# One kernel, two plans: W_in block 3 of the first pair moved to the split path, W_out low parts built by SyncE copies and adding transfers

## The chip, the cores and the metric

The kernel runs on one core of one Trainium2 chip. The metric is the device time of one execution in microseconds (us); before the change it is 329.56 us, the median of three runs (329.25 to 329.67). The engines are TensorE (PE in the profile; PEld are its weight loads), VectorE (DVE), ScalarE (ACT), GpSimd (POOL) and SyncE (SP), which does nothing here but issue transfers. Each engine works through its own instructions strictly in the order in which the program lists them; engines wait for each other by semaphores.

## The reference

A Mamba-2 scan over 4 batches, 8 heads and 768 steps is followed by a feed-forward block with SiLU over the 3072 resulting rows. Everything is fp32.

```python
# scan, per batch and head, in chunks of 32 steps
L = np.exp(cum[:, :, :, None] - cum[:, :, None, :]) * causal
M = np.einsum('bhin,bhjn->bhij', Cc, Bc) * L
y_intra = np.einsum('bhij,bhjd->bhid', M, xc)
y_inter = np.einsum('bhin,bhnd->bhid', Cc, state) * np.exp(cum)[:, :, :, None]
y[:, :, sl] = y_intra + y_inter
state = decay_full[:, :, None, None] * state + np.sum(Bx, axis=2)
...
# feed-forward, x: (3072, 256), w_in: (256, 2048), w_out: (2048, 256)
h = x @ w_in
g = h * (1.0 / (1.0 + np.exp(-h)))
out = g @ w_out
```

## The kernel before

**Units and pairs.** The 3072 rows are cut into 12 units `u` of 256 steps (three for each batch). The scan runs unit by unit; two units make a pair `P` or `G`, and the feed-forward block runs pair by pair, on 512 columns at a time.

**An order written out by hand.** The whole program is one list of entries, `SCHEDULE`, read from left to right: a name and up to four numbers, looked up in `DO` and called. An entry appends its instructions to the lists of its engines. So the list sets the order on each engine, and the order between engines only where data is handed over. A second table, `SLOTS`, says which buffer of a pool each new tile takes; a tile that takes a used buffer has to wait for the last reader of the tile before it. There is no scheduler that could move anything later.

**The weights.** `W_in` and `W_out` are each cut into eight blocks of 256 features; blocks 0 to 7 are W_in, 8 to 15 are W_out. A block is loaded (`lw`) as raw bits, and ACT (`u`, `v`), DVE (`w`, three steps) and POOL (`W`) make an fp32 tile of it (`WT`, 128 x 512). For the fast path a block is split into three tiles: a high part (`H`, ACT), a low part and a third part. The low part is "high + WT". For ten blocks DVE adds it up (`lD`, line 326). For the other six (10 to 15) ACT first copies the high part into a new tile (`Wl`, line 335), and then a transfer issued by POOL adds WT to it in place (`Wm`, line 339, `accum_op=ALU.add`). The third part is made by DVE (`dD`) or by ACT and a second adding transfer (`Wd`, `We`).

**Two ways through the matrix products.** In the split path a product is three sums of TensorE passes over fp32r tiles, each instruction one record in the trace: `a` (high and low parts, 8 records, into PSUM bank `ga` for even blocks and `gb` for odd ones), then ACT scales that bank (`ax`), then `d` (third part, 4 records), then ACT applies SiLU (`dg`). `h` (ACT), `l` and `e` (DVE) split the activations, and `q` is the second product (one `q` is three records). In the plain path fp32 tiles are used as they are, and TensorE takes two records for each instruction: `s` is the first product of one unit and one block (8 records of 256 columns), `si` its SiLU, and `n1` the second product (2 records of 512 columns). Only the first pair (units 0 and 1) uses the plain path: its blocks 0 to 5 in `s`, its blocks 6 and 7 in `a` and `d`, and all its second products in `n1`. The 32 `n1` are ready early and stand in the list where TensorE would otherwise wait.

**The scan of a unit** is, in order: the loads (`Ln` B rows, `Lt` B and C for a transpose, `La` the decays, `Lp` their prefix products, `Lx` the unit's x in two halves), all issued by SP; two transposes on DVE (`T`); a running product on DVE (`E`, two halves); `B` and `C` on POOL; `g0` and `gd` on TensorE (`gd` reads both x halves); two small copies out of PSUM on ACT (`b`); state sums on DVE (`S`); two masked copies on ACT (`SM`); a product on DVE (`M`); then `Y` on TensorE, which needs all of these; `y` and `xh` on ACT, `x` on DVE, which split the unit's result for the feed-forward block. Units 2, 4, 6 ... share one buffer of x (`xt`), units 3, 5, 7 ... another, and all units from 2 on share one B tile (`bn`) and one tile for the transposes (`tbc`). So a unit's loads may only be issued when the unit that used the buffer before is done with it.

**The queues.** SP issues all loads and all output stores in the order of the list, and a transfer that has to wait for a buffer or for its source holds back all that stand behind it. POOL's queue carries `W`, `B`, `C`, the small stores of the decays (`AD`) and the adding transfers. The lines that the change and the prediction's steps touch:

- line 326 `lD`, line 330 `dD`, line 322 `H`, line 335 `Wl` and `Wd`, line 339 `Wm` and `We`
- line 269 `Lx`, line 254 `Ln`, line 262 `Lt`, line 229 `La`, line 237 `Lp`
- line 697 `s`, line 703 `si`, line 761 `n1`, line 782 `q`, line 800 `a` and `d`, line 811 `ax`, line 821 `dg`, line 827 `h`
- line 585 `g0`, line 571 `gd`, line 594 `b`, line 615 `S`, line 623 `SM`, line 600 `M`, lines 635 and 644 `Y`, line 672 `y`, line 679 `xh`, line 318 `W`, line 520 `B`

Of the kernel before, what the change touches and what calls it, by code (L numbers as in the profile page):

```python
# [8 lines left out]
FP32 = mybir.dt.float32  # L9
# [30 lines left out]
n1,2,0 W,11 H,10 a,1,0 Wl,10 Wm,10 n1,3,1 n1,4,0 Lt,4,1,2,0 T,4,1 x,3,1 si,1,3 S,3,3 Lp,4,0 C,4 ce,4,1 E,4,0 H,11 ax,1,0  # L40
d,1,0 E,4,1 ce,4,0 Lt,4,0,2,0 n1,5,1 Wl,11 Lx,5,1,0 Wl,13 dg,1,0 n1,4,1 T,4,0 H,8 lD,1 Ln,4,0,0,0 g0,4 lD,2 Ln,4,0,1,0
B,4 H,9 M,4,1 La,5,1,0 Wm,11 Lx,4,1,0 Wm,12 gd,4 b,4,0 lD,8 b,4,1 dD,1 n1,6,1 h,1,0 S,4,0 S,4,1 Lx,5,0,0 H,3 S,4,2
SM,4,1 n1,14,0 n1,6,0 SM,4,0 Lt,5,1,3,0 M,4,0 n1,7,0 Vn,0 Y,4 y,4,1 y,4,0 xh,4 l,1,0 n1,7,1 S,4,3 a,1,2 Vn,1 lD,9 dD,8
dD,2 H,5 a,1,1 ax,1,2 e,1,0 q,1,0,1,0 d,1,2 dD,9 q,1,0,0,1 Ln,5,0,0,0 ax,1,1 d,1,1 Wd,13 Lt,5,1,1,0 q,1,0,0,0 q,1,0,1,1
AD,3 Lt,5,1,0,0 dD,4 dg,1,2 Lt,5,0,3,0 h,1,2 a,1,4 dg,1,1 h,1,1 Lt,5,1,2,0 T,5,1 ce,5,0 Lt,5,0,2,0 ce,5,1 Lt,5,0,0,0
lD,3 a,1,3 Lp,6,0 dD,10 o,0,1,2 We,12 dD,3 x,4,1 x,4,0 l,1,2 e,1,2 ax,1,4 d,1,4 H,14 q,1,2,0,1 Ln,5,0,1,0 ax,1,3 d,1,3
l,1,1 La,5,0,0 E,5,0 dg,1,4 e,1,1 q,1,1,1,1 dg,1,3 Lt,5,0,1,0 h,1,3 q,1,1,0,1 E,5,1 T,5,0 g0,5 B,5 M,5,1 Lp,5,0 C,5 gd,5
b,5,1 lD,5 Lt,6,1,0,0 b,5,0 S,5,0 Lt,6,1,3,0 S,5,1 Wm,13 We,13 dD,5 q,1,2,1,1 La,6,0,0 q,1,2,0,0 a,1,5 Lx,6,1,0 Wl,14
ax,1,5 M,5,0 q,1,1,1,0 l,1,3 S,5,2 q,1,1,0,0 SM,5,1 dD,11 La,6,1,0 e,1,3 SM,5,0 d,1,5 h,1,4 dg,1,5 h,1,5 o,0,0,2
Lt,6,1,2,0 Lt,6,1,1,0 T,6,1 q,1,2,1,0 l,1,4 e,1,4 q,1,3,0,0 l,1,5 e,1,5 q,1,3,1,0 Wd,15 Y,5 E,6,1 Lt,6,0,1,0 y,5,0 y,5,1  # L50
xh,5 q,1,3,1,1 q,1,3,0,1 ce,6,0 Lt,6,0,0,0 a,1,7 ce,6,1 q,1,4,0,0 q,1,5,1,0 Lt,6,0,3,0 ax,1,7 q,1,4,1,0 Lt,7,1,1,0 Wm,15
# [76 lines left out]
def kernel(  # L128
# [145 lines left out]
    WF = 256  # L274
# [614 lines left out]
```

## Time and profile before

| | us | share of the span |
|---|---|---|
| median of three runs | 329.56 | |
| profiled execution, whole | 329.1 | |
| profiled execution, span of its instructions | 327.4 | |
| PE busy | 320.3 | 98% |
| DVE busy | 240.4 | 73% |
| ACT busy | 209.5 | 64% |
| POOL busy | 56.0 | 17% |
| mean granted TensorE clock | | 0.999 |

The profile is of one execution. Its span runs from the first to the last instruction, and 1.7 us of the execution's time lie around it. Rows give a line of the kernel, an engine, an operation and the tiles written and read; buffer numbers are left out, so all tiles of a pool have one name (`s2k`, `r4k`, `raw` and the PSUM pool `hp`). A row of groups gives count, busy time, the mean of one in ns, the idle time of the engine just before them and what ended it. A row of the timeline or of the chain gives start and duration in us. "SPq" and "PEq" are queues: an engine's sequencer that issues or waits.

DVE and the DMA engines are at their fullest in the first third of the span, where weights are prepared and the scan of units 0 to 4 runs; the page's rows of 40 slices show DVE at nine tenths or more in eight of the ten slices from the second to the eleventh. The same rows show the DMA engines at six tenths or more in eleven of the first thirteen slices.

### The profile page before, as it was taken

What the parts mean: (1) busy time and instruction counts of PE and PEld (TensorE: products, weight loads), DVE (VectorE), ACT (ScalarE), POOL (GpSimd) and SP (SyncE); (2) the same over time, 40 slices, a digit from 0 to 9 for tenths busy, and PEclk for the clock granted to TensorE, in tenths of its full rate; (3) what the DMA queues carried; (4) which work ended last, traced back from release to release, by engine and by line L of the source; (5) the groups of instructions that cost most, each with busy time, mean ns of one, the idle gap of its engine ahead of it and who ended that gap; (6) DMA issues with size and microseconds to landing.
All of it is one profiled execution on the core that took longest, in us unless ns stands there. A gap on an engine that the chain in (4) does not pass through costs nothing.

```text
span 327.4 us, 7519 instructions
## 1 busy us (share of the span) xinstructions
PE 320.3 (98%) x3064; PEld 243.4 (74%) x3067; DVE 240.4 (73%) x331; ACT 209.5 (64%) x319; POOL 56.0 (17%) x74
## 2 busy tenths in 40 slices
PE   8999999999999999999999999999999999999994
PEld 3478576655687777878887778878887788888883
DVE  4998999999988965877687299665787544635553
ACT  4679978648696846583771875837775455574641
POOL 1364766326102330001200010010001000000000
PEclk9999999999999999999999999999999999999999
DMA  6979966479872663423633306514042000050003
GB/s 162 206 200 272 296 175 192 51 148 135 148 127 46 105 115 53 86 36 64 147 74 70 44 1 117 104 26 96 3 74 37 7 2 2 0 88 0 2 1 64
DMA packets 94962, 29.27 MB, mean 89 GB/s; under 512 B 80000, under 2 KB 86912, under 8 KB 94928
## 3 DMA queue, kind: packets, MB, share of 16 engines
q1 hardware_dynamic: 90960, 25.71, 37.5%
q0 software_dynamic: 1616, 2.82, 5.1%
q10 hardware_dynamic: 2352, 0.26, 0.6%
q8 instruction: 24, 0.39, 0.5%
q14 instruction: 10, 0.08, 0.1%
HBM read 22.81 MB, written 3.34 MB: 80 GB/s over the span
## 4 chain that ended last, share of the span: by engine, by line
PE 94%; SPq 2%; DMA 1%; DVE 1%; issue 1%; DVEq 0%
PE hp L782 29%; PE ga L800 18%; PE gb L800 18%; PE hp L761 9%; PE hp L697 6%; PE o_ps L782 6%; PE ga L635 2%; PE ga L585 2%; PE ga L644 2%; DMA s2k<-in_C_dram 1%; PE gb L644 1%; PE ga L571 1%; SPq L262 0%; SPq L375 0%; PE o_ps L531 0%
## 5 line engine op out<-in xcount | busy, mean ns | idle before, releaser
L782 PE MATMUL hp<-r4k,s2k 128*128 128x512 f32 x400 | 110.0, 394 | 0.0
L651 DVE SCALAR_TENSOR_TENSOR r4k<-r4k,r4k 128x1024 fp32r<-128x1024 f32 (+1 forms) x42 | 50.5, 1202 | 51.3 <-ACT r4k L827 48.2
L782 PEld LDWEIGHTS hp<-r4k,s2k 128*128 128x128 f32 x400 | 74.0, 188 | 16.4 <-issue 0.3
L800 PE MATMUL ga<-raw,s2k 128*128 128x512 f32 x240 | 62.3, 395 | 0.0
L800 PE MATMUL gb<-raw,s2k 128*128 128x512 f32 x240 | 61.1, 390 | 0.0
L800 PEld LDWEIGHTS ga<-raw,s2k 128*128 128x128 f32 x240 | 44.7, 188 | 11.4 <-ACT ga L811 0.9
L800 PEld LDWEIGHTS gb<-raw,s2k 128*128 128x128 f32 x240 | 44.8, 188 | 9.9 <-ACT gb L811 0.5
L837 DVE SCALAR_TENSOR_TENSOR r4k<-r4k,r4k 128x1024 fp32r<-128x1024 f32 x40 | 49.2, 1231 | 3.4 <-DVE r4k L651 0.9
L827 ACT ACTIVATE r4k<-r4k 128x1024 fp32r<-128x1024 f32 x40 | 42.2, 1058 | 3.2 <-issue 1.3
L811 ACT ACTIVATE ga<-ga 128x1024 f32<-128x1024 f32 x21 | 21.1, 1007 | 24.6 <-PE ga L800 23.8
L811 ACT ACTIVATE gb<-gb 128x1024 f32<-128x1024 f32 x21 | 21.2, 1009 | 17.6 <-PE gb L800 13.3
L782 PE MATMUL o_ps<-r4k,s2k 128*128 128x512 f32 x80 | 30.7, 390 | 0.0
L761 PE MATMUL hp<-r4k,s2k 128*128 128x512 f32 x64 | 30.0, 602 | 0.0
L821 ACT ACTIVATE r4k<-gb 128x1024 f32<-128x1024 f32 x21 | 21.4, 1021 | 12.4 <-PE gb L800 9.9
L520 POOL TENSOR_TENSOR BT<-bn,ab 128x256 f32<-128x256 f32 x10 | 6.7, 672 | 129.5 <-DVE ab L512 123.3
L318 POOL TENSOR_TENSOR s2k<-s2k,s2k 128x512 uint32<-128x512 uint32 (+1 forms) x19 | 23.6, 1250 | 26.4 <-DVE s2k L307 13.7
L821 ACT ACTIVATE r4k<-ga 128x1024 f32<-128x1024 f32 x21 | 21.5, 1023 | 8.4 <-PE ga L800 8.2
L512 DVE TENSOR_TENSOR_SCAN ab<-ab,diag 128x512 f32<-128x512 f32 x20 | 24.8, 1265 | 0.0
L697 PE MATMUL hp<-r4k,s2k 128*128 128x256 f32 x96 | 22.3, 382 | 0.2 <-issue 0.2
L697 PEld LDWEIGHTS hp<-r4k,s2k 128*128 128x128 f32 x96 | 18.0, 190 | 4.0 <-issue 1.4
L761 PEld LDWEIGHTS hp<-r4k,s2k 128*128 128x128 f32 x64 | 11.6, 189 | 10.5 <-issue 9.6
L782 PEld LDWEIGHTS o_ps<-r4k,s2k 128*128 128x128 f32 x80 | 15.0, 188 | 3.2
(123 smaller groups left out, 384.8 us busy)
## 6 DMA issues: line engine op xcount, KB each, us to landing
ab<-az SPq DMA_DIRECT2D x20, 256.0 KB, 4.2
raw<-in_moe_w_in_dram SPq DMA_DIRECT2D x8, 512.0 KB, 4.2
raw<-in_moe_w_out_dram SPq DMA_DIRECT2D x8, 512.0 KB, 8.0
out_dram<-r4k SPq DMA_DIRECT2D x44, 64.0 KB, 2.0
xt<-in_x_dram SPq DMA_DIRECT2D x20, 128.0 KB, 4.2
s2k<-s2k POOLq DMA_DIRECT2D x10, 256.0 KB, 3.8
pfx<-ac SPq DMA_DIRECT2D x10, 130.0 KB
bn<-in_B_dram SPq DMA_DIRECT2D x20, 64.0 KB, 5.2
```

The source lines that it names most:

```text
L318: nc.gpsimd.tensor_tensor(out=u[:, :, fs], in0=u[:, :, fs], in1=v[:, :, fs], op=ALU.add)
L512: nc.vector.tensor_tensor_scan(out=o, data0=src, data1=diag.rearrange("p h t -> p (h t)"), initial=0.0, op0=ALU.mult, op1=ALU.add)
L644: nc.tensor.matmul(out=y[w][32 * q:32 * q + 32, c, 64 * k:64 * k + 64], lhsT=xc[64 * c:64 * c + 64, k, h], rhs=m[64 * c:64 * c + 64, k, h] ...
L651: nc.vector.scalar_tensor_tensor(out=l, in0=f32(h), scalar=BACK, in1=y, op0=ALU.mult, op1=ALU.add)
L697: nc.tensor.matmul(out=hp[:, i], lhsT=WT[j][:, kc, 128 * i:128 * i + 128], rhs=XM()[:, 2 * kc:2 * kc + 2, u], start=(kc == 0), stop=(kc == ...
L761: nc.tensor.matmul(out=NP[m], lhsT=WT[8 + f // 2][:, f % 2, 128 * m:128 * m + 128], rhs=GT[0, f // 2][:, f % 2], start=(n == 1), stop=(n = ...
L782: nc.tensor.matmul(out=ACC[P, c], lhsT=WK[8 + i, p][:, k, 128 * m:128 * m + 128], rhs={"h": HT, "l": LT, "d": DT}[p][P, i][:, k], start=(n ...
L800: nc.tensor.matmul(out=o, lhsT=WK[j, q][:, kc, 128 * i:128 * i + 128], rhs=xs[:, 2 * kc:2 * kc + 2], start=(start and q == "h" and kc == 0 ...
L811: nc.scalar.activation(t, t, AF.Copy, scale=1.0 + Z)
L821: nc.scalar.activation(g, t, AF.Silu, scale=BACK)
L827: nc.scalar.activation(t, GT[G, i], AF.Copy, scale=-LESS * Z)
L837: nc.vector.scalar_tensor_tensor(out=DT[G, i], in0=f32(HT[G, i]), scalar=-1.0, in1=f32(LT[G, i]), op0=ALU.mult, op1=ALU.subtract)
```

## The change

The first 200 of the 1309 entries stay as they are. From there the list is a new one of 1111 entries, with new tables of buffers. As sets of entries, the old and the new list differ in this:

- `s,0,3`, `s,1,3`, `si,0,3`, `si,1,3` go; `a,0,3`, `ax,0,3`, `d,0,3`, `dg,0,3` come. Block 3 of W_in for the first pair is then computed in the split path, as blocks 6 and 7 are. Its three weight parts were made before too, for the later pairs; in the new list they are made earlier.
- `Wl` of blocks 10 to 15 (copies by ACT) and `lD` of blocks 8 and 9 (sums by DVE) go. For all eight W_out blocks SP copies the high part into the tile of the low part (`Wc`), and an adding transfer from POOL's queue (`Wm`) adds WT to it; `Wm` of blocks 8 and 9 is new.
- All other entries are the same ones, in a new order from the 201st on.

Two functions for a spill to memory (`f_ds`, `f_dl`) are defined and not called.

```diff
+    def w_copy(n):
+        t = WK[n, "l"] = small(f"l{n}", [128, 2, WF], FR)
+        nc.sync.dma_start(out=f32(t).rearrange("p k f -> p (k f)"), in_=f32(WK[n, "h"]).rearrange("p k f -> p (k f)"))
...
-        "Wl": lambda n: w_part(n, "l"), "Wd": lambda n: w_part(n, "d"), "Wm": lambda n: w_more(n, "l"),
+        "Wl": lambda n: w_part(n, "l"), "Wd": lambda n: w_part(n, "d"), "Wc": w_copy, "Wm": lambda n: w_more(n, "l"),
```

The part of the two lists around units 3 and 4, of which the prediction speaks. Before:

```
M,3,1 Lx,3,0,0 gd,3 b,3,0 b,3,1 S,3,0 S,3,1 Lt,4,0,1,0 w,9,2 n1,0,0 n1,14,1 Lx,4,0,0 Lt,4,0,0,0 La,4,0,0 S,3,2 W,9
n1,13,1 SM,3,0 M,3,0 SM,3,1 lD,0 Y,3 n1,2,1 n1,3,0 Lt,4,0,3,0 dD,0 La,4,1,0 w,11,0 w,11,1 y,3,0 y,3,1 xh,3 x,3,0 w,11,2
n1,2,0 W,11 H,10 a,1,0 Wl,10 Wm,10 n1,3,1 n1,4,0 Lt,4,1,2,0 T,4,1 x,3,1 si,1,3 S,3,3 Lp,4,0 C,4 ce,4,1 E,4,0 H,11 ax,1,0
d,1,0 E,4,1 ce,4,0 Lt,4,0,2,0 n1,5,1 Wl,11 Lx,5,1,0 Wl,13 dg,1,0 n1,4,1 T,4,0 H,8 lD,1 Ln,4,0,0,0 g0,4 lD,2 Ln,4,0,1,0
B,4 H,9 M,4,1 La,5,1,0 Wm,11 Lx,4,1,0 Wm,12 gd,4 b,4,0 lD,8 b,4,1 dD,1 n1,6,1 h,1,0 S,4,0 S,4,1 Lx,5,0,0 H,3 S,4,2
SM,4,1 n1,14,0 n1,6,0 SM,4,0 Lt,5,1,3,0 M,4,0 n1,7,0 Vn,0 Y,4
```

After:

```
n1,1,1 n1,13,1 b,3,0 S,3,0 b,3,1 S,3,1 S,3,2 SM,3,0 M,3,0 lD,0 SM,3,1 La,4,0,0 Lx,4,0,0 Y,3 H,2 x,2,1 Lt,4,1,1,0
Lt,4,1,2,0 lw,11 v,11 Lt,4,0,1,0 x,2,0 y,3,1 n1,4,1 W,9 dD,0 n1,3,0 n1,3,1 w,11,2 y,3,0 xh,3 x,3,0 a,1,0 H,9 u,11 H,15
Lt,4,1,0,0 n1,4,0 Wm,8 Lt,4,1,3,0 n1,2,0 La,4,1,0 Wc,13 ax,1,0 T,4,1 x,3,1 Wc,9 d,1,0 ce,4,0 ce,4,1 Ln,4,0,0,0 w,11,0
w,11,1 W,11 E,4,0 Lt,4,0,0,0 n1,6,1 Wm,9 dg,1,0 n1,7,1 Lt,5,1,2,0 Ln,4,0,1,0 H,11 Lp,4,0 E,4,1 Lt,4,0,2,0 Lt,4,0,3,0
T,4,0 g0,4 B,4 Lt,5,1,3,0 lD,1 S,3,3 Lx,4,1,0 Ln,5,0,1,0 AD,2 gd,4 b,4,0 S,4,0 M,4,1 n1,6,0 b,4,1 h,1,0 S,4,1 S,4,2
M,4,0 n1,5,0 H,5 La,5,0,0 n1,2,1 C,4 SM,4,0 Ln,5,0,0,0 lD,2 dD,2 l,1,0 SM,4,1 Vn,1 Y,4
```

The entries around the low parts of blocks 12 and 14 in the new list (entries in between left out):

```
We,13 ... Wc,12 ... Wm,12 ... B,6 ... La,7,1,0 ... We,15 ... Wc,14 ... Lt,7,1,0,0 ... C,6 ... Lx,7,0,0 ... Wm,14 We,14 ... We,12 La,7,0,0 ... Lt,7,1,3,0 T,7,1
```

And around unit 10:

```
O,2,0,2,3,0 SM,9,0 Y,9 ... La,11,0,0 ... O,0,1,2,2,0 ... Lt,11,1,1,0 ... O,2,1,2,1,0 Lt,10,0,1,0 Lt,10,0,2,0 ... Lt,10,0,3,0 Lt,10,0,0,0 T,10,0 g0,10 Lx,10,0,0 gd,10
```

More of the change, by code (lines that the diff above doesn't have):

```diff
@@ L755, with f_ds, f_dl @@
     NP = {}
+    def f_ds(i):
+        spill[i] = dram.tile([128, 1024], FP32, name=f"spill{i}")
+        nc.sync.dma_start(out=spill[i], in_=GT[0, i].rearrange("p k n -> p (k n)"))
+    def f_dl(i):
+        g = GT[0, i] = large(f"R0_{i}", [128, 2, 512])
+        nc.sync.dma_start(out=g.rearrange("p k n -> p (k n)"), in_=spill[i])
+    spill = {}
     def f_n(f, m):
```

151 lines of the change are left out of this document (73 added, 78 removed), and 6 rows, old and new, of the table SLOTS.

## The prediction, made before the changed kernel ran

> **What bounds the kernel now.** I read the page's busy times and chain first, then the busy time by stretches, then the chain in order of time, and last the queues that feed TensorE.
>
> ```profile
> span 327.4 us, 7519 instructions
> PE 320.3 (98%) x3064; PEld 243.4 (74%) x3067; DVE 240.4 (73%) x331; ACT 209.5 (64%) x319; POOL 56.0 (17%) x74
> PE 94%; SPq 2%; DMA 1%; DVE 1%; issue 1%; DVEq 0%
> ...
> 0.00:20.00 20.00, 17.66 (x224) 9.82 (x234) 15.29 (x39) 11.73 (x25) 6.60 (x18) 1.00 0.80 174
> 20.00:60.00 40.00, 39.72 (x353) 28.16 (x353) 37.01 (x60) 32.43 (x61) 23.05 (x26) 1.00 0.84 228
> 60.00:90.00 30.00, 30.00 (x480) 17.99 (x479) 29.18 (x44) 19.56 (x41) 10.64 (x12) 1.00 0.70 121
> ```
>
> TensorE is the bound. The chain that ended last is 94% PE, and PE is busy 98% of the span. The rows by stretches (length, then PE, PEld, DVE, ACT, POOL busy, clock, DMA share, GB/s) say where it is not: 2.3 us of the first 20, which lie inside the 200 entries that the change keeps, and almost nothing from 20 to 90 us, although DVE and the DMA engines are nearly full there too (29.18 of 30.00 us, and a share of 0.70). The clock is whole, so the clock explains nothing. Two things follow. Time can only be won by taking work off PE, about as much as is taken off. Time can be lost anywhere where PE's next instruction comes to stand behind a late producer, because PE has no idle time left to absorb it.
>
> **The change part by part.** *PE's own work.* Two entries "s" (block 3, one per unit of the first pair) go; one "a" and one "d" come.
>
> ```profile
> 51.48 1.73 PE hp L697 x8
> ...
> 88.51 1.82 PE gb L800 x8
> ...
> 90.34 0.68 PE hp L782 x3
> 91.02 0.91 PE ga L800 x4
> ```
>
> One "s" is 8 records in 1.73 us, one "a" 8 in 1.82, one "d" 4 in 0.91. So PE loses 2 x 1.73 = 3.46 us and gains 2.73: **-0.7 us**. Everything else on PE is the same set of entries in another order.
>
> *Work off the other engines.*
>
> ```profile
> L335 ACT ACTIVATE s2k<-s2k 128x512 fp32r<-128x512 f32 x10 | 6.2, 625 | 0.1
> L326 DVE TENSOR_TENSOR s2k<-s2k,s2k 128x512 fp32r<-128x512 f32 x10 | 7.5, 756 | 0.0
> L703 ACT ACTIVATE r4k<-hp 128x512 f32<-128x512 f32 x12 | 7.1, 589 | 2.6 <-PE hp L697 2.6
> L811 ACT ACTIVATE ga<-ga 128x1024 f32<-128x1024 f32 x21 | 21.1, 1007 | 24.6 <-PE ga L800 23.8
> L821 ACT ACTIVATE r4k<-ga 128x1024 f32<-128x1024 f32 x21 | 21.5, 1023 | 8.4 <-PE ga L800 8.2
> L339 POOL DMA_DIRECT2D s2k<-s2k x10 | 8.8, 935 | 12.9 <-DMA s2k<-s2k 5.8 <-ACT s2k L335 3.7 <-issue 3.4
> ```
>
> ACT loses six "Wl" (6 x 0.625) and two "si" (2 x 0.589) and gains "ax" and "dg" (1.007 + 1.023): -2.9 us. DVE loses two "lD" (2 x 0.756): -1.5 us. POOL gains two adding transfers (2 x 0.935): +1.9 us on an engine that is busy 10.64 of the 30 us where they fall. All three sums I cost at nothing: PE's unbroken work covers them. Without that cover, relief of ACT would be worth at most its 2.9 us.
>
> *The copies on SyncE.* Eight copies of 256 KB enter SP's queue, which also issues every load in order. No row shows such a copy. Its landing lies between the x load's shortest 3.0 us and the longest adding transfer's 5.9 us (rows below; the adding transfer has the same tile, shape and both ends in SBUF); I take that transfer's median, 3.8. The low parts are first used many microseconds after their transfers land, so their own latency costs nothing. What costs is what stands **behind** them. A copy "Wc,n" waits for "H,n" on ACT. For blocks 8, 13, 10, 11 and 15 "H" stands far earlier in the order, so these do not hold the queue. "Wc,12" and "Wc,14" reuse buffers that earlier adding transfers read, and wait for those; behind "Wc,14" stand the loads of unit 7, first used by the transposes of unit 7 some 16 us of PE entries later, by the prices above: nothing again. "Wc,9" is different. "H,9" stands on ACT directly behind "xh,3", which needs "Y,3" of unit 3, and nine transfers later in SP's queue comes "Lx,4,1", the second half of unit 4's x, which "gd,4" on PE needs. The rows of before for these same steps:
>
> ```profile
> 66.08 0.38 PE ga L571 x32
> 66.46 2.77 PE hp L761 x6
> 69.23 0.20 PE ga L635 x2
> ...
> 77.85 1.72 PE hp L761 x4
> ...
> 80.18 0.39 PE ga L571 x32
> 80.57 3.63 PE hp L761 x8
> ```
>
> ```profile
> 68.31 0.64 ACT L623 ACTIVATE sm<-st,par 128x96 f32<-128x96 f32 x2 [1.28 <-DVE st L615]
> 70.49 0.38 ACT L672 ACTIVATE ys<-ga 128x256 f32<-128x256 f32 x1 [1.54 <-PE ga L644]
> 71.18 0.63 ACT L679 ACTIVATE raw<-ys 128x512 fp32r<-128x512 f32 x1
> 71.72 0.61 ACT L322 ACTIVATE s2k<-s2k 128x512 fp32r<-128x512 f32 x1
> ```
>
> ```profile
> 64.40 0.33 SPq L262 DMA_DIRECT2D tbc<-in_B_dram  x1
> ...
> 70.61 0.38 SPq L269 DMA_DIRECT2D xt<-in_x_dram  x1
> 71.09 1.31 SPq L254 DMA_DIRECT2D bn<-in_B_dram  x2
> 72.50 0.60 SPq L229 DMA_DIRECT2D ab<-az  x1
> 73.16 2.29 SPq L269 DMA_DIRECT2D xt<-in_x_dram  x2
> ...
> 79.28 0.37 SPq L254 DMA_DIRECT2D bn<-in_B_dram  x1
> 79.70 1.05 SPq L262 DMA_DIRECT2D tbc<-in_C_dram  x2
> 80.85 0.70 SPq L262 DMA_DIRECT2D tbc<-in_B_dram  x1
> ...
> SPq L262 <- DMA tbc<-in_B_dram: 3.0, 3, 1.5
> ...
> L269 SPq DMA_DIRECT2D xt<-in_x_dram x20: 375/474/1658, 40.7 to 244.0; - x20
> DMA to landing us min/median/max: 3.0/4.2/5.3
> ...
> DMA to landing us min/median/max: 3.3/3.8/5.9
> ```
>
> The first landing row is that of x, the last that of the adding transfers. Now the steps. (1) *Unit 3.* Up to "Y,3" the new order holds one n1 (half of the 1.72 row, 0.86) more and the 0.7 less: +0.1. Between "gd,3" and "Y,3" it holds two n1 instead of three. Before, the path from "gd,3" over the small copies, the state sums and the two "SM" to "Y,3" took 2.77 us behind L571's end, three n1 being 2.58, so PE lost 0.2. In the new order one VectorE step of about 0.6 us ("w,9,2") no longer stands in that path, which makes it 2.15 against 1.72 of cover: 0.4 lost, **+0.2** more than before (-0.2 to +0.4). "Y,3" then starts at 69.23 + 0.1 + 0.2 = 69.5. (2) "H,9". Before, the ACT step right behind "xh,3" ended at 71.72 + 0.61 = 72.33; with the shift of 0.3, "Wc,9" goes out at about 72.7. Until then SP holds back everything behind it. (3) Nine issues to "Lx,4,1". Nine steps of the run that began at 64.40 ended at 70.61: 0.69 each; three after the idle stretch, 79.28 to 80.85, took 0.52 each. I take 0.58, between the two as the run starts on empty queues and then fills them (SP's waits for earlier landings, 3.0 us in 3 places, are that filling): 72.7 + 5.2 = 77.9; by the ends 77.4 and 78.9. (4) Landing by 4.2 us: 82.1; by 3.0 from the early end 80.4, by 5.3 from the late end 84.2. (5) PE. Between "Y,3" and "gd,4" stand the same entries in number (seven n1, one "a", one "d", one "g0"), so "gd,4" is reached 80.18 - 69.23 = 10.95 us after "Y,3", at 80.5, and its second half, which reads the late tile, at 80.7. So PE stands for **1.4 us** (-0.3, which is no stall, to 3.5). Before, the same load was issued at 73.16 and could not be late: 73.16 + 5.3 is 78.5.
>
> [...]
>
> (6) *Unit 4's "Y".* Three n1 cover it instead of four, and ACT has one "h" and one "H" in that path:
>
> ```profile
> L827 ACT ACTIVATE r4k<-r4k 128x1024 fp32r<-128x1024 f32 x40 | 42.2, 1058 | 3.2 <-issue 1.3
> L322 ACT ACTIVATE s2k<-s2k 128x512 fp32r<-128x512 f32 x16 | 9.7, 624 | 1.0 <-POOL s2k L318 1.0
> ```
>
> Two small copies (about 0.6 with their start), 1.06, 0.62, two "SM" (0.7) and the hand-over 0.15: 3.1 us against 2.58 of cover, 0.5 lost where the row of before (3.63 for four n1 of 0.86) lost 0.2: **+0.35** (0 to +0.7). (7) *Unit 10.* "La,11,0" waits on SP for "Y,9", and eight issues behind it comes the x of unit 10, with 8.1 us of PE entries between "Y,9" and "gd,10" (seven "q" of 0.68, an "a", a "d", a "g0" of 0.6): 8 x 0.5 to 8 x 0.69 plus 3.0 to 5.3 is 7.0 to 10.8, with the middle values 8.8. The other x half and most other loads of that unit are issued ahead, and the queue is empty there (DMA share falls after 90 us), so I take the low side: **+0.2** (0 to 2).
>
> Sum: -0.7 + 0.2 + 1.4 + 0.35 + 0.2 = **+1.45 us** on the profiled execution's 329.1 us (span 327.4, and 1.7 around it): 330.55. The median of the three runs, 329.56, lies 0.46 above the profiled one, so I predict **331.0**.
>
> **The rivals.** *No hold* (0.20): "Wc,9" delays the queue but the transfers come through at 0.52 a piece and 3.0 us, so "gd,4" is not late. Then -0.7 + 0.2 + 0.35 and perhaps unit 10: 329.4 for the median, between 328.7 and 330.0. For it: the shortest landing and the fast run of issues do exist. Against it: both would have to hold in the stretch with the fullest DMA. *The relief of ACT and DVE decides* (0.13), the faster side: ACT is busy 32.43 and DVE 37.01 of the 40 us from 20 to 60, and the small waits of PE end on them. If 2.9 and 1.5 us less of their work removes those waits (the 0.28 us of that row and the 0.2 each at units 3 and 4) and no hold appears, 0.7 + 0.7 us are won: 328.2, between 327.9 and 328.9. It decides if the late x lands before 80.5. *The hold is worse* (0.15): the copy lands after 5.9 us instead of 3.8; the transfer eight places behind it waits for that landing, and unit 4's transposes and x come 2 us later still, or unit 10 pays its full 2 us: 332.5 to 334.5.
>
> **How the numbers follow.** The forecast has 0.52; its own range, from stalls of 0.5 to 2.8 us at "gd,4", is 330.2 to 332.4. The range for 8 in 10 takes in most of "no hold" and part of the worst case: 328.7 to 333.0. A change under 0.2% (0.66 us) can hardly be told from none. Faster than 328.9: all of the relief case and a fourth of "no hold", 0.18. Within: the rest of "no hold" and the low end of the forecast, 0.20. Slower: 0.62.
>
> **What would show it.** Right: SP standing some 3 us before a copy at 72 to 73.5 us, released by the ACT line of "H"; the x load of unit 4 issued at 77 to 79; PE idle over 1 us ahead of L571's counterpart near 80.5, waiting for x; PE's "s" records down from 96 to 80 and "a" and "d" up by 12; total PE work 0.7 us lower. Wrong: that x load issued before 76, or PE without a gap there (then "no hold" or the relief); a gap elsewhere, above all around the unit-6 low parts of blocks 12 and 14, which I cost at nothing.

## The result, and the profile after

The changed kernel is slower. Its median is 333.42 us over 14 runs (331.91 to 336.83), that of the kernel before in the same comparison 329.61 over 14 (328.43 to 332.3); the ratio is 1.0125, with a 95% interval of 1.0106 to 1.0144. The profiled execution took 331.91 us (span 330.2). Two runs of the experiments below, 335.86 in e14 and 336.87 in e18, are counted as slow and stay out of the ratios, though not out of the medians.

The page of the changed kernel: span, TensorE's busy time, the chain that ended last by engine, and two groups that answer to the change (busy us, mean ns; and KB and median us to landing of the SyncE copies).

```profile
span 330.2 us, 7524 instructions
...
PE 319.6 (97%) x3060; PEld 241.9 (73%) x3063; DVE 236.3 (72%) x329; ACT 207.9 (63%) x313; POOL 59.2 (18%) x76
...
PE 77%; DVE 7%; DMA 5%; SPq 4%; POOL 2%; issue 2%; ACT 1%; DVEq 0%; ACTq 0%
...
L701 PE MATMUL hp<-r4k,s2k 128*128 128x256 f32 x80 | 18.4, 381 | 0.2 <-issue 0.2
...
s2k<-s2k SPq DMA_DIRECT2D x8, 256.0 KB, 4.2
```

Its busy times by stretches, with the columns that were used before:

```profile
20.00:60.00 40.00, 38.97 (x433) 27.28 (x419) 34.56 (x58) 29.53 (x56) 23.34 (x24) 1.00 0.72 197
60.00:90.00 30.00, 28.26 (x379) 16.14 (x380) 24.44 (x40) 19.56 (x39) 11.41 (x12) 1.00 0.85 171
```

TensorE has 0.7 us less work (320.3 to 319.6; 80 records of "s" instead of 96), and VectorE and ScalarE have less too. Yet TensorE now stands 1.0 us between 20 and 60 us and 1.7 between 60 and 90, where it stood 0.3 and 0.0. The chain, 94% TensorE before, is 77% TensorE, and the rest passes through VectorE, loads, SyncE and GpSimd. (Up to line 335 the changed kernel has the line numbers of before; from there on they are 4 higher, and 14 higher from "n1" on. The experiments have up to 2 more.)

TensorE's records were put beside the entries of the order, one group to each entry, to see where the time between two entries grew. The places, from the start of "a,0,7" to the start of the last product, a stretch of 292.0 us (before: 288.7):

| place | TensorE stands | what was late |
|---|---|---|
| a,0,6 at 45 us | +1.1 us | the low part of block 6 |
| n1 ahead of Y,3 | +0.2 | unit 3's state sums |
| ahead of g0,4 at 80 us | +0.7 | unit 4's transposes, behind block 9's copy on SyncE |
| inside gd,4 at 82 us | +1.25 | unit 4's x, behind the same copy |
| ahead of g0,11 at 255 us | +0.7 | VectorE, which stood for an output store |
| work | -0.7 | block 3 |

The two figures ahead of a "g0" hold some 0.1 us that every step to a "g0" takes, before the change too; without it the places add up to 3.1 of the 3.3 us. The hold on SyncE, which the prediction is about, in SyncE's rows in order of time (start, us):

```profile
69.35 5.07 SPq L339 DMA_DIRECT2D s2k<-s2k  x2
...
78.92 0.43 SPq L269 DMA_DIRECT2D xt<-in_x_dram  x1
```

in its waits between 66 and 84 us (us in total, times, longest):

```profile
SPq L339 <- ACT s2k L322: 3.9, 1, 3.9
```

and in the chain of waits:

```profile
78.92 4.20 DMA xt<-in_x_dram
83.17 0.35 PE ga L575 x16
```

Block 13's copy and block 9's make one row of 5.07 us, of which 3.9 are the wait for "H,9" (L322 on ScalarE). The x load leaves at 78.92, lands 4.20 us later, and the second 16 products of "gd,4" start at 83.17. The wait that was not foreseen, in the chain of the same profile 35 us earlier:

```profile
40.81 0.89 POOL ac L474
41.70 0.03 issue
41.72 2.72 POOL s2k L318
44.45 0.02 issue
44.47 0.64 ACT s2k L322
45.11 0.02 issue
45.13 1.85 DVE s2k L326
46.99 0.04 issue
47.03 1.66 PE ga L814 x6
```

"W,6" on GpSimd (L318) takes 2.72 us; "H,6" follows on ScalarE, "lD,6" on VectorE takes 1.85, and "a,0,6" on TensorE, which began at 45.15, goes on only at 47.03. In the kernel before the add also stands behind a store of the prefix sums, and counted from "a,0,7" it began only 0.5 us earlier. Its row there, and two rows of VectorE, the step beside the add and the low part of block 6:

```profile
41.70 1.28 POOL L318 TENSOR_TENSOR s2k<-s2k,s2k 128x512 uint32<-128x512 uint32 x1
...
41.72 1.55 DVE L303 TENSOR_SCALAR s2k<-s2k 128x512 f32<-128x512 f32 x1 [0.33 <-ACT s2k L294]
...
44.73 0.68 DVE L326 TENSOR_TENSOR s2k<-s2k,s2k 128x512 fp32r<-128x512 f32 x1
```

So the add's place in its own queue is not what differs, but what ran beside it. Before, the add began first and took 1.28 us, and VectorE's step beside it took 1.55, where the median of that line is 0.42. In the changed kernel four steps of VectorE followed each other from 41.61 to 43.30 and the add, begun among them, took 2.72; then GpSimd's next add began at 45.00, and the low part beside it took 1.85 instead of 0.68. Each time the step that began later was the one that took longer. In the experiment below where the same add has VectorE idle beside it, it takes 1.27 us.

The last place of the table, ahead of "g0,11", goes back to VectorE (start, us, and in brackets the idle time before with what ended it): "l,4,2" takes a buffer that an output store still reads.

```profile
248.71 1.23 DVE L655 SCALAR_TENSOR_TENSOR r4k<-r4k,r4k 128x1024 fp32r<-128x1024 f32 x1 [3.63 <-DMA out_dram<-r4k]
...
255.13 0.62 DVE L529 STREAM_TRANSPOSE bh<-tbc 128x256 f32<-128x256 f32 x1
```

VectorE loses 3.63 us, so the transpose for "g0,11" ends at 255.75 and TensorE stands ahead of it.

One more thing belongs to the result: a run's time goes with its granted clock. Over all comparisons the changed kernel has a median of 333.2 us in 11 runs with a clock of 0.997 or more and 334.8 in 9 below; the kernel before 329.6 in 53 and 331.1 in 15.

### The profile page after: what moved, and what is told of

Same layout as the page of the kernel before. It is cut to its first block, busy times and chain, and to the rows that moved or that the text cites. A ratio compares the mean times of both kernels' runs of the same rounds, so it can differ in the third digit from the quotient of the medians.

```text
span 330.2 us, 7524 instructions
## 1 busy us (share of the span) xinstructions
PE 319.6 (97%) x3060; PEld 241.9 (73%) x3063; DVE 236.3 (72%) x329; ACT 207.9 (63%) x313; POOL 59.2 (18%) x76
## 4 chain that ended last, share of the span: by engine, by line
PE 77%; DVE 7%; DMA 5%; SPq 4%; POOL 2%; issue 2%; ACT 1%; DVEq 0%; ACTq 0%
PE hp L796 26%; PE ga L814 16%; PE gb L814 16%; PE o_ps L796 5%; PE hp L775 4%; PE hp L701 3%; DMA xt<-in_x_dram 3%; DMA s2k<-in_B_dram 2%; PE ga L589 2%; PE ga L639 1%; POOL s2k L318 1%; PE ga L648 1%; DVE r4k L655 1%; SPq L262 1%; PE ga L575 1%
## 5 line engine op out<-in xcount | busy, mean ns | idle before, releaser
L796 PEld LDWEIGHTS hp<-r4k,s2k 128*128 128x128 f32 x400 | 74.0, 188 | 16.4 <-issue 0.3
L825 ACT ACTIVATE gb<-gb 128x1024 f32<-128x1024 f32 x22 | 22.2, 1008 | 20.5 <-PE gb L814 20.5
L318 POOL TENSOR_TENSOR s2k<-s2k,s2k 128x512 uint32<-128x512 uint32 (+1 forms) x19 | 25.0, 1322 | 26.9 <-DVE s2k L307 17.2
L835 ACT ACTIVATE r4k<-gb 128x1024 f32<-128x1024 f32 x22 | 22.5, 1024 | 10.6 <-PE gb L814 8.0
L524 POOL TENSOR_TENSOR BT<-bn,ab 128x256 f32<-128x256 f32 x10 | 7.7, 770 | 107.7 <-DVE ab L516 86.0
L516 DVE TENSOR_TENSOR_SCAN ab<-ab,diag 128x512 f32<-128x512 f32 x20 | 25.9, 1308 | 0.0
L775 PEld LDWEIGHTS hp<-r4k,s2k 128*128 128x128 f32 x64 | 11.6, 189 | 9.8 <-issue 8.4
L701 PE MATMUL hp<-r4k,s2k 128*128 128x256 f32 x80 | 18.4, 381 | 0.2 <-issue 0.2
L701 PEld LDWEIGHTS hp<-r4k,s2k 128*128 128x128 f32 x80 | 15.0, 190 | 3.1 <-issue 0.9
```

The lines of the kernel that those rows point to most:

```text
L318: nc.gpsimd.tensor_tensor(out=u[:, :, fs], in0=u[:, :, fs], in1=v[:, :, fs], op=ALU.add)
L516: nc.vector.tensor_tensor_scan(out=o, data0=src, data1=diag.rearrange("p h t -> p (h t)"), initial=0.0, op0=ALU.mult, op1=ALU.add)
L524: nc.gpsimd.tensor_tensor(out=BT[u][:, ks], in0=bn[u][:, ks], in1=E[u][:, ks, :, Q - 1:Q].to_broadcast([128, n, H, N]), op=ALU.mult)
L701: nc.tensor.matmul(out=hp[:, i], lhsT=WT[j][:, kc, 128 * i:128 * i + 128], rhs=XM()[:, 2 * kc:2 * kc + 2, u], start=(kc == 0), stop=(kc == ...
L775: nc.tensor.matmul(out=NP[m], lhsT=WT[8 + f // 2][:, f % 2, 128 * m:128 * m + 128], rhs=GT[0, f // 2][:, f % 2], start=(n == 1), stop=(n = ...
L796: nc.tensor.matmul(out=ACC[P, c], lhsT=WK[8 + i, p][:, k, 128 * m:128 * m + 128], rhs={"h": HT, "l": LT, "d": DT}[p][P, i][:, k], start=(n ...
```

## The experiments

Short names e1 to e18 stand for the labels. Each edit is in the written order of the changed kernel, if it isn't said otherwise, and each tile keeps its buffer. "To the last product" is the stretch from "a,0,7" as above, read in the profile of each. Ahead of it, the stretch up to "a,0,7", nearly the same in all, varied from 32.7 to 34.7 us (once 37.7), so single profiles are compared by the stretch behind it.

**Do the waits repeat?** No edit.

> The changed kernel once more, to see which of its waits repeat. Theory 'two late producers': TensorE again stands in front of a,0,6 (about 1.1 us, low part of block 6 late), ahead of g0,4 (0.7) and inside gd,4 (1.25, x of unit 4 late), about 3.1 us in all, at the same places; ratio to the kernel before 1.010 to 1.015. Rival 'scattered': the waits stand elsewhere or have other sizes by more than half, because the extra transfers disturb the run at random; then the profiled span also differs by over 1 us from 330.2. The 0.7 us ahead of g0,11 is expected to be gone if it was chance.

> The kernel before, profiled once more, for what its first profile cannot tell alone: how far one order differs from run to run. From a,0,7 to the last product 288.7 us in the first profile, and no wait of TensorE over 0.5 us between; expected again within 0.5. The stretch up to a,0,7, the same entries in both kernels, took 33.1 us there and 32.7 to 34.7 in the nine profiles of the changed order and its variants: if it is again 33.1 or less, the changed order also costs about 0.6 us there; if it is 33.5 or more, that stretch merely varies.

The changed kernel: median 333.54, ratio 1.0107 (1.0067 to 1.0148); a,0,6 +0.9, g0,4 +0.7, gd,4 +1.2, g0,11 +0.8, and a new one of 0.8 at "q,1,6", where the third part of block 14 of W_out, the last link of its copy and two adding transfers, was late; 293.0 us to the last product. The kernel before: 288.4, no wait over 0.5, and 33.6 us up to "a,0,7". So the waits belong to the order, that of g0,11 too; the start merely varies, and the first profile of the changed kernel (32.7) had the shortest one of all.

**Take block 9's copy out of the way.** Three ways. In e2 copy and adding transfer go behind the x load, and "dD,9" and "dD,8" change places:

```diff
-x,3,1 Wc,9 d,1,0
+x,3,1 d,1,0
...
-n1,6,1 Wm,9 dg,1,0
+n1,6,1 dg,1,0
...
-Lx,4,1,0 Ln,5,0,1,0 AD,2
+Lx,4,1,0 Ln,5,0,1,0 Wc,9 Wm,9 AD,2
```

In e5 the copy stands as in e2, the adding transfer further back, and "dD,9" behind "dD,1":

```diff
-SM,4,1 Vn,1
+SM,4,1 Wm,9 Vn,1
...
-a,1,2 dD,1 ax,1,2
+a,1,2 dD,1 dD,9 ax,1,2
```

In e13 ScalarE makes the copy, in its place:

```diff
-x,3,1 Wc,9 d,1,0
+x,3,1 Wl,9 d,1,0
```

> Only the copy of block 9 (and its adding transfer) is put behind the x load of unit 4 on SyncE. Theory 'hold': the waits ahead of g0,4 and inside gd,4 go, 1.9 to 2.0 us, so about 331.4 and a ratio of 1.005 to 1.007; the x load goes out before 76 us. Rival 'the copies slow the transfers in general': the same copy still runs among the loads, x lands late all the same, and less than 0.6 us is won (ratio 1.011 to 1.014). Rival 'next wait': TensorE reaches Y,4 earlier and stands there instead; 0.5 to 1.2 us won.

> Block 9's copy behind unit 4's x on SyncE as in the earlier run, but its adding transfer now behind GpSimd's step C of unit 4 (there it stood ahead of it and waited for the copy), and the third part of block 9 later on VectorE. Theory 'hold': no wait ahead of g0,4, in gd,4 or ahead of Y,4 beyond 0.5 us; from a,0,7 to the end about 295.6 us against 297.5 to 298.5 of the changed kernel; median 331.5, ratio 1.005 to 1.007. Rival 'TensorE waits at Y,4 in any case' (its VectorE and ScalarE steps take longer than the cover, whatever SyncE does): 1 to 2.4 us stay at Y,4 and under 1 us is won (ratio over 1.009).

> The changed order with one edit: the low part of block 9 is copied by ScalarE (0.625 us) instead of SyncE, at its place; the other seven copies stay on SyncE. Theory 'one hold': the waits ahead of g0,4 and in gd,4 go (1.95 us), the rest of the changed kernel's waits stay; a,0,7 to the end about 290.0 us, median 331.5. Rival 'eight copies crowd the queue': unit 5's loads still come late behind the other copies, TensorE waits 0.8 to 1.8 us at a,1,3 or g0,5 as it did when the copy was moved behind x; a,0,7 to the end over 290.8.

e2: 335.39, ratio 1.0164 (1.0123 to 1.0205). The waits of g0,4 and gd,4 are gone, and 2.4 us stand ahead of "Y,4" instead. The chain of that place in e4, which has the same edit (start, us, piece):

```profile
80.34 3.17 DMA s2k<-s2k
...
83.54 0.02 POOLq L345
...
84.09 0.53 POOL s2k L345
...
84.70 0.91 POOL ac L476
85.61 0.72 POOL cw L557
```

The adding transfer (L345) waits on GpSimd for the copy to land, and behind it on the same queue stands step C of unit 4 (L557), which "Y,4" needs: the edit's own fault. e5 mends it: nothing stands at g0,4, gd,4 or Y,4 any more, 1.8 us are won up to there, but the median is 334.56, ratio 1.0152 (1.0128 to 1.0176). Ten us later TensorE stands 0.5 and 1.3 us at "a,1,4" and "a,1,3". The chain of e5:

```profile
88.96 0.65 SPq L264
...
89.65 4.73 DMA tbc<-in_C_dram
...
94.60 0.67 DVE ct L531
```

A small load of unit 5, issued behind three copies, lands after 4.73 us; VectorE stands for it with its whole queue, and what "a,1,3" and "d,1,4" need comes late. Then 1.7 us at "q,1,6". e13 has the copy of block 9 on ScalarE, and seven on SyncE: 331.62, ratio 1.0068 (1.0042 to 1.0094), 290.9 to the last product. No wait at unit 4 or 5. So the loss there is that one copy, as e13's first theory said (the 290.9 lie just above the 290.8 that the rival named, but the waits that it foresaw are not there); moving it back in SyncE's queue only moved the loss to the next load.

**How can x be late, if it goes out at the same time?** In e13 the x load left at 79.58, hardly earlier than in the changed kernel counted from "a,0,7" (45.9 against 46.25), and TensorE passed "gd,4" without a wait. Rows of SyncE and TensorE in e13:

```profile
79.58 0.43 SPq L271 DMA_DIRECT2D xt<-in_x_dram  x1
...
82.23 0.45 PE L577 MATMUL ga<-xt,BT 64*32 64x64 f32 x32
```

All 32 products run from 82.23, so x had landed after some 2.8 us at most, against 4.20. The reason why x leaves hardly earlier stands in SyncE's waits between 69 and 81 us, here of e13 and of e7 (below, all eight copies on ScalarE):

```profile
SPq L264 <- DVE ct L531: 2.2, 1, 2.2
...
SPq L264 <- DVE ct L531: 4.0, 1, 4.0
```

Without the copy's wait SyncE stands at the third load behind it ("Lt,5,1,2,0") for a transpose on VectorE. Counted from "a,0,7" that load goes out 1.1 us earlier than in the changed kernel, in e13 and in e7, and x 0.35 us earlier in e13 and 1.25 in e7. So of the 3.9 us for which the copy held the queue, about 1 is its price; the rest the queue would have stood anyway.

e17 asks why x needed 4.20 us; it leaves the copy, and moves the adding transfer that went out 0.8 us ahead of x ("dD,9" again behind "dD,1").

```diff
-n1,6,1 Wm,9 dg,1,0
+n1,6,1 dg,1,0
...
-SM,4,1 Vn,1
+SM,4,1 Wm,9 Vn,1
```

> The changed order with block 9's copy left where it is; only its adding transfer goes to a later place (behind step C of unit 4 on GpSimd, with block 9's third part later on VectorE). In the changed kernel the adding transfer goes out 0.8 us ahead of unit 4's x load, which then lands after 4.2 us; where copy or adding transfer come later, x is not late although it goes out at nearly the same time. Theory 'hold': x goes out at the same time and lands after 4 us, the wait in gd,4 stays over 1 us. Rival 'traffic': with 256 KB less ahead of it x lands in under 3 us, the wait in gd,4 falls under 0.4 us, and only the one ahead of g0,4 (0.7) stays.

Rows of SyncE and TensorE in e17:

```profile
69.94 5.12 SPq L341 DMA_DIRECT2D s2k<-s2k  x2
...
79.56 0.43 SPq L271 DMA_DIRECT2D xt<-in_x_dram  x1
...
82.55 0.46 PE L577 MATMUL ga<-xt,BT 64*32 64x64 f32 x32
```

SyncE is held as long (5.12) and x leaves as late, but it has landed by 82.7. So "traffic" is right for gd,4, and "hold" for g0,4, whose 0.8 us stay. In e13 the same adding transfer went out 0.1 us ahead of x and x was not late; with the lead of 0.8 us TensorE stood in gd,4 in e1, e3 and e8 too, 1.2 to 1.3 us. The prediction priced x at the row's median landing, 4.2 us. The load needed 4.20 us in the changed kernel and at most 3.1 in e17. The median did not gain by it, 333.35 (ratio 1.0115, 1.0083 to 1.0146): in the profile TensorE then stands 1.7 us in the middle of "Y,4", up to 88.36, and the trace names no releaser for it. It may be a wait for instructions, which have a DMA queue of their own in the profile (packets, MB, share of the span):

```profile
q8 instruction: 24, 0.39, 0.5%
```

The 24 packets are of 16 KB each. That they are TensorE's is an estimate of mine: its 6123 records in the changed kernel (3060, and 3063 weight loads) would make 255 to a packet. e18 has a wait without a releaser too, 2.18 us in the middle of "Y,1", up to 28.37; between that place and the one in "Y,4" TensorE has some 1260 records in the changed kernel's trace, about five packets by this estimate. From 24 to 34 us TensorE is idle for 0.8 to 1.5 us in e2, e6, e8, e10 and e12 as well, and for 0.16 at most in e1, e9 and the first profiles of the two kernels; that is part of why the stretch ahead of "a,0,7" varies. No run tests it.

**Bring block 6's add forward**, alone (e3), with e2's edit (e4), with e13's (e14).

```diff
-n1,11,1 AA,1 AP AD,1 s,1,1 si,1,1 Ln,2,1,1,0 w,6,2 W,6 H,6 Lx,2,1,0
+n1,11,1 w,6,2 W,6 H,6 AA,1 AP AD,1 s,1,1 si,1,1 Ln,2,1,1,0 Lx,2,1,0
```

> Only the last three steps that make block 6's high part (w,6,2, W,6, H,6) are put ahead of the prefix step on GpSimd and VectorE. Theory 'late low part': the wait inside a,0,6 goes, 1.1 us, so about 332.3 and a ratio of 1.008 to 1.010, with the add of block 6 starting near 39 us. Rival 'moved wait': the prefix sums leave GpSimd 1.5 to 2.7 us later, unit 2's loads of them land later, and TensorE waits as long at g0,2 or gd,2 (ratio 1.011 to 1.014).

> Both moves together. If the two late producers are all that the change costs in the profiled run: 3.1 us less than the changed kernel, about 330.3, ratio 1.001 to 1.004. If the part of the median that the profiled run did not show (1.5 us against 0.5 before) hangs on the same waits: 329.0 or less, ratio 0.995 to 1.000. If the added transfers cost by themselves: over 331.5, ratio above 1.006.

> The last kernel with block 6's add early as well. 'Two late producers': 1.1 us less again, a,0,7 to the end about 288.9 us, median 330.4, ratio 1.001 to 1.004, as much as with all eight copies on ScalarE (288.9 us). Rival 'eight copies crowd the queue': over 290 us, ratio over 1.005.

The add in e3, in GpSimd's row, now with VectorE idle beside it:

```profile
40.68 1.27 POOL L320 TENSOR_TENSOR s2k<-s2k,s2k 128x512 uint32<-128x512 uint32 x1 [1.10 <-DVE s2k L312]
```

In all three the wait at "a,0,6" is gone (2.24 us from its start to that of the next group, instead of 3.37). What follows differs. e3: 334.0, ratio 1.0116 (1.0075 to 1.0156); its profile has 291.7 to the last product, no more than 0.3 to 1.3 below the changed kernel, as g0,3, Y,3 and g0,4 stand 0.1 to 0.3 longer, and four of its six runs have a clock of 0.991 or 0.992. e4: 333.74, ratio 1.0128 (1.0073 to 1.0183), with e2's wait at Y,4. e14: 331.64, ratio 1.0057 (1.0034 to 1.008), over e13 nothing that can be told; 289.9 to the last product, with a new 0.5 at g0,3. The wait is explained by its place, its price is not won back in full.

**Move three causes at once** (e6: e5's edit, block 6's add, and one "q" ahead of g0,11).

```diff
-T,11,0 dg,4,5 h,4,5 Ln,11,0,0,0 g0,11 B,11
+T,11,0 dg,4,5 h,4,5 Ln,11,0,0,0 q,4,3,0,1 g0,11 B,11
```

> The clean hold move, the early add of block 6, and one q (q,4,3,0,1) put ahead of g0,11, where TensorE stood 0.7 to 0.8 us in each profile. Theory 'the late producers are the whole loss': 1.95 + 1.1 + 0.7 = 3.75 us less than the changed kernel; a,0,7 to the end about 293.9 us (before: 294.3), median 329.7, ratio 0.997 to 1.002. Rival 'the transfers cost in general': ratio stays above 1.005 with waits spread over new places.

332.65, ratio 1.0101 (1.0071 to 1.0131); 290.7 to the last product. e5's wait at "a,1,3" (0.9) stays, and the 0.7 at g0,11 only moves to "a,4,4". The late step there is VectorE's, and e18 takes its wait away at the source; both stores leave their later places:

```diff
-O,2,0,2,0,0 dg,4,0
+O,2,0,2,0,0 O,2,0,2,2,0 O,2,0,2,1,0 dg,4,0
```

> The changed order with two output stores of pair 2 issued some 20 entries earlier on SyncE. In the changed kernel VectorE stands 3.6 us for the landing of such a store, whose buffer the low part of pair 4's block 2 takes, and is then late with unit 11's transpose. Theory 'store holds VectorE': the wait ahead of g0,11 (0.7 to 0.8 us in three profiles) falls under 0.3 us and the time by 0.5 us (ratio 1.008 to 1.011). Rival 'VectorE is full there anyway': VectorE no longer stands for the store but the wait ahead of g0,11 stays over 0.5 us.

The row of "l,4,2" in e18, whose profile is of the longest of its six runs:

```profile
253.34 1.23 DVE L656 SCALAR_TENSOR_TENSOR r4k<-r4k,r4k 128x1024 fp32r<-128x1024 f32 x1 [2.69 <-ACT r4k L842]
```

It waits for its own input instead of the store, and no wait is left ahead of g0,11 (from "Y,10" to "g0,11" 18.0 us instead of 18.7 and 18.8). The median, 334.1 (ratio 1.0107, 1.0072 to 1.0143), does not show half a microsecond: the six runs lie between 331.7 and 336.87.

**All eight copies on ScalarE.** In e7 each "Wc" is a "Wl" in its place. e10 has e3's edit besides, and the adding transfer of block 15 behind step B of unit 5; e16 also has one n1 ahead of "Y,3":

```diff
-Wm,15 ce,5,0 g0,5 Lx,5,0,0 B,5 gd,5
+ce,5,0 g0,5 Lx,5,0,0 B,5 Wm,15 gd,5
...
-n1,13,1 b,3,0
+n1,13,1 n1,4,1 b,3,0
```

> The order of the changed kernel, only the eight copies of SyncE made by ScalarE instead (0.625 us each), at the same places of the order. Theory 'hold': SyncE no longer stands in front of block 9's copy, so g0,4 and gd,4 wait no more (1.9 us); Y,4 may wait up to 1.2 us as ScalarE has one step more ahead of it; a,0,6 and g0,11 keep their 1.1 and 0.7; ratio 1.004 to 1.009. Rival 'the copies are harmless, the order alone costs': the waits at unit 4 stay over 1.2 us and the ratio 1.010 to 1.014. Rival 'ScalarE becomes the bound': ratio above 1.014.

> The copies on ScalarE in the changed order (332.15 us in the last set), with block 6's add early and the adding transfer of block 15 behind step B of unit 5, ahead of which it stood and held GpSimd for 0.8 us. Theory 'late producers': 1.1 + 0.8 us less, a,0,7 to the end about 289.4, median 330.2, ratio 1.001 to 1.005. Rival 'next wait': each producer that comes in time only shows the next late one; less than 0.8 us won, ratio over 1.006.

> All copies on ScalarE, block 6's add early, block 15's adding transfer behind step B of unit 5, and n1,4,1 moved ahead of Y,3, where 0.35 to 0.5 us of wait stood. Sum of the parts: a,0,7 to the end 288.9 - 0.35 = 288.5 us, no better than the kernel before within what can be measured (ratio 0.998 to 1.003). Rival: the n1 is missed ahead of g0,4 and the wait stands there; 288.9.

e7: 332.15, ratio 1.0089 (1.0063 to 1.0116). The waits of unit 4 are gone, 0.8 us stand ahead of gd,5, as the adding transfer of block 15 now waits on GpSimd ahead of step B. e10: 331.18, ratio 1.0027 (1.0002 to 1.0053), 288.9 to the last product, and the chain of its page is TensorE's again:

```profile
span 328.5 us, 7520 instructions
...
PE 92%; SPq 3%; DMA 2%; DVE 1%; issue 1%; ACT 0%; DVEq 0%
```

Three causes taken away bring back most of the loss. e16: 332.13, ratio 1.0059 (1.0036 to 1.0083); Y,3 waits no more, 0.9 and 0.6 us stand at "q,1,3" and "q,1,5" instead. No version beat the kernel before.

**One part of the change alone, in the order of the kernel before.** In e12 each of the six "Wl" is a "Wc". e11 and e15 have block 3's form; TensorE's entries around unit 3 in e15:

```diff
-n1,15,0 s,0,3 n1,13,0 Y,2 n1,5,0 s,1,3 g0,3 gd,3 n1,0,0 n1,14,1 n1,13,1 Y,3
+n1,15,0 n1,0,0 n1,13,0 Y,2 n1,5,0 a,0,3 n1,14,1 n1,13,1 d,0,3 g0,3 gd,3 n1,14,0 n1,4,0 Y,3
```

"H,3", "lD,3" and "dD,3" come early enough for them, in the buffers of "H,15", "Wl,15" and "H,13", which go later with "lD,4", "Wl,13" and "Wd,13". e11 has "n1,5,0" where e15 has "n1,0,0", the other way round behind "Y,2", and leaves "lD,4" and "H,15" where they were.

> The order of the kernel before with only its six low-part copies moved from ScalarE to SyncE, each at its place in the order. Theory 'the copies crowd SyncE': the copy of block 10 waits for its high part behind unit 3's xh and holds the loads of unit 4 behind it, so TensorE waits 1 to 3 us between g0,4 and Y,5; ratio 1.003 to 1.010. Rival 'only the new order costs': the copies are as harmless as on ScalarE, which is relieved by 3.75 us; ratio 0.997 to 1.001.

> The order of the kernel before with only block 3's form changed (a and d between Y,2 and g0,3, six n1 moved forward to cover; its H, lD, dD take the buffers that the low part of block 15 and the high part of block 13 had, which come later). Theory 'PE price of the parts': 0.7 us less work, waits of 0 to 0.4 us at Y,2 or Y,3; a,0,7 to the end 288.0 to 288.4, ratio 0.996 to 1.000. Rival 'the order has no slack': earlier lD,3 and dD,3 make VectorE late for unit 3 or 4, over 1 us of new waits, ratio over 1.002.

> Block 3's form alone in the order of the kernel before, once more: this time n1,0,0 (not n1,5,0, which came ahead of its own block's add and waited 3.3 us) takes the place of the first s, and the low part of block 4 gives up its early place on VectorE to block 3's. Theory 'PE price of the parts': a,0,7 to the end 287.7 to 288.2 us against 288.4 and 288.7 of the kernel before; ratio 0.996 to 1.000. Rival 'no slack on VectorE': 0.5 to 1.5 us of waits between Y,2 and g0,4; ratio 1.000 to 1.005.

e12: 342.32, ratio 1.0347 (1.030 to 1.0393). The waits between 76 and 92 us, and the stretches (columns as before):

```profile
POOL BT L526 <- DMA bn<-in_B_dram: 6.8, 1, 6.8
...
PE ga L577 <- POOL BT L526: 4.2, 1, 4.2
```

```profile
86.00:88.00 2.00, 0.05 (x7) 0.00 (x0) 0.00 (x0) 0.00 (x0) 0.00 (x0) 1.00 0.92 161
88.00:90.00 2.00, 0.00 (x0) 0.00 (x0) 0.00 (x0) 0.00 (x0) 0.40 (x1) 1.00 0.83 130
...
92.00:94.00 2.00, 2.00 (x3) 0.67 (x2) 1.85 (x6) 2.00 (x5) 0.60 (x1) 0.50 1.14 214
94.00:96.00 2.00, 2.00 (x4) 0.85 (x3) 2.00 (x4) 0.05 (x1) 0.00 (x0) 0.50 0.77 154
```

A load that stands behind copies on SyncE stops GpSimd, and with it TensorE, for 4.2 us; TensorE then runs at half the clock for 6.8 us. So the copies are the dangerous part; in the order of the changed kernel it is mainly one of the eight that costs (e13). e11 (340.55, ratio 1.031, 1.027 to 1.0349) and e15 (338.33, 1.0245, 1.0221 to 1.0269) say less than they should. e11's n1,5,0 came ahead of the add of its own block, 3.3 us; in e15 VectorE (two scans in one row of 3.39 us) brings block 3's low part late, 1.5 us at "a,0,3", and the parts that I put off stand on ScalarE in front of "ax,1,3", 2.5 us. They show that the early order has no room for block 3's parts, and not what its form is worth. The reverse test, block 3 split again in the changed kernel:

```diff
-a,0,3 ax,0,3 d,0,3 dg,0,3
+s,0,3 si,0,3 s,1,3 si,1,3
```

Each stands in the place of the one that it replaces.

> Only the changed form of block 3 undone: its a, ax, d, dg of the first pair are again s, si for each unit, at the same places. Theory 'PE price of the parts': 2 x 1.73 instead of 1.81 + 0.91, so 0.7 us longer than the changed kernel, waits unchanged: a,0,7 to the end about 298.4, ratio 1.012 to 1.015. Rival 'the split form is what costs': the time falls by 0.5 us or more (ratio under 1.009).

335.01, ratio 1.0168 (1.0142 to 1.0195), 1.5 us more than the changed kernel where 0.7 was expected. Beside the work, its profile has a halved clock behind the waits at unit 4. Stretches of e8, and below them those of the changed kernel:

```profile
82.00:84.00 2.00, 0.98 (x49) 0.67 (x48) 1.50 (x3) 0.00 (x0) 0.73 (x2) 1.00 1.21 163
84.00:86.00 2.00, 1.38 (x18) 0.82 (x19) 0.61 (x2) 0.93 (x3) 0.00 (x0) 0.84 1.14 200
86.00:88.00 2.00, 2.00 (x3) 0.67 (x2) 1.95 (x5) 1.56 (x4) 0.00 (x0) 0.50 0.98 253
```

```profile
82.00:84.00 2.00, 0.98 (x34) 0.50 (x19) 0.20 (x2) 0.38 (x3) 0.00 (x0) 1.00 1.12 191
84.00:86.00 2.00, 2.00 (x6) 0.74 (x4) 1.97 (x6) 2.00 (x5) 0.00 (x0) 1.00 0.74 171
```

The same two waits, 0.8 and 1.25 us, cost 1.9 us more in e8 (n1 of 1.45, 1.71 and 1.31 us instead of 0.86) and nothing more in the changed kernel's own profile.

## Why the prediction was right and wrong

*Right in place and size, but only half in its mechanism: the hold.* The copy of block 9 waits 3.9 us for "H,9" (about 3 foreseen), x leaves at 78.92 (77.9; 77.4 to 78.9), lands after 4.20 (4.2), and TensorE stands 1.25 us in gd,4 (1.4). The steps came out some 1.0 us later, since the wait at a,0,6 had moved everything. With that copy on ScalarE (e13), or its adding transfer later (e17), the wait is gone. "No hold" and "relief of ACT and DVE decides" are out. But step (2) took the copy's wait as all that holds x back, and without it x would have left only 0.35 (e13) to 1.25 us (e7) earlier, as SyncE stands there for a transpose too. Step (4) did not ask why x takes 4.2 us: the adding transfer of the same block went out 0.8 us ahead. So that the stall came out near 1.4 is partly luck. And step (2) named only x among the transfers held back; the B and C loads that unit 4's transposes need stood in the same queue, 0.6 us ahead of g0,4.

*Right: TensorE's work*, 0.7 us less, and unit 3, 0.2 us more as foreseen. *Wrong but small:* (6) and (7) did not come; Y,4 waits as before and unit 10 not at all, so 0.55 us of the sum was not there. (The low end of the forecast's own range, 330.2, is 330.1 by its own terms; nothing hangs on it.)

*Wrong: the step at which the relief of the other engines was "costed at nothing" because "PE's unbroken work covers them".* With it the whole rest of the new order had no term: the sum prices units 3, 4 and 10 and no other place. I took the early waits of TensorE as something that could only vanish or stay, as PE had no idle time there. But at a,0,6 the cover was too short. The new order set block 6's add and low part beside other steps of VectorE and GpSimd, they took 2.72 and 1.85 us instead of 1.28 and 0.68, and TensorE lost 1.1 us. That the late add is the cause is shown by e3, e4, e6, e10 and e14, which put it forward and have no wait there; that the two engines held each other up is read from the rows and not tested by itself. And at 255 us, 34 us behind unit 10, the last place that I had priced, a buffer shared with an output store cost 0.6 (shown by e18). With the 0.6 at g0,4 that is 2.3 us not in the sum: 1.45 - 0.55 + 2.3 is 3.2 us, and the stretch behind "a,0,7" grew by 3.3. The result lies in the range of "the hold is worse", but not by its mechanism: unit 10 waited for nothing, and x landed after 4.2 us as forecast.

*Wrong: the step from the profiled execution to the median*, 0.46 us as before. It was 1.5; of the 2.4 us between the forecast's 331.0 and the result this step has 1.0, and the sum above 1.4. The changed kernel's profile had the shortest start of all (32.7 us up to "a,0,7"; the next one 33.4), and its median run has more of what its profile lacks: a clock under 0.997 in 9 of 20 runs (before: 15 of 68), worth 1.6 us. That such runs hold a halved clock behind one of the waits is argued from e2, e8, e12 and e18, whose profiles show it there; no profile of the changed kernel itself has one.

*Open.* Whether the wait in the middle of "Y,4" in e17 is one for instructions. What sets a run's clock: which wait halves it, and in which runs. Why e14 and e18, with a wait less, have medians that do not show it. And what block 3's form would bring with an order made for it: its price on TensorE is measured, -0.7 us, its cost on the others only in orders that had no place for it.

## What to carry to other kernels

When the bound engine is busy 98%, price a reordering by producers and not by sums: for each instruction on the bound engine ask when its last input is made now and in the new order, and follow that from the first changed entry to the last, stores and shared buffers too. A transfer put into an in-order queue that also issues loads costs what stands behind it, and it can cost twice: by the wait of its issue, as far as the queue would not have stood anyway (about 1 of 3.9 us here), and by the traffic that comes with it ahead of the next load (x landed after 4.20 us with block 9's adding transfer 0.8 us ahead, after 3.1 at most without it). Take one such cause away and the next late producer can appear within ten microseconds, as in e2 and e5, so test fixes together before calling a cause small.

## What the runs showed of the hardware

- TensorE's clock fell to 0.50 for 3.4 us behind short waits: in e8 behind 0.8 and 1.25 us of standing within 3 us, in e2 behind 2.4 us; in e12 behind 4.2 us, for 6.8 us there. The same waits left it at 1.00 in other profiles: the two in the changed kernel's, the one of e2 in e4's. So the same waits cost nothing in one run and 1.9 us in another, and no run shows what decides it.
- A 256 KB transfer between SBUF buffers, plain on SyncE or adding on GpSimd, lands after about 4.2 and 4.3 us (medians of the changed kernel), and an x load issued 0.8 us behind an adding one needed 4.20 us, without it 3.1 at most.
- An integer add of two 128x512 tiles on GpSimd and VectorE's steps on tiles of that size took longer beside each other, on either engine: the add took 2.72 us among four steps of VectorE that had begun first, 1.28 us where it had begun first itself (VectorE's step then took 1.55 instead of 0.42), and 1.27 us beside an idle VectorE.
